# A routed layer whose next tokens are turned at the beginning of a slot instead of among its output products

## The chip, the cores and the metric

The kernel runs on one core of one Trainium2 chip. The metric is the device time of one execution in microseconds (us); the kernel before was run three times. Beside those runs one execution was taken by the hardware profiler; all rows below are from it, and their times count from the start of its span. Engines are called as in the profile: PE multiplies matrices, PEld loads its weights, DVE and ACT are the vector and the scalar engine, POOL is the general-purpose engine (here it mostly issues gathers and scatters), SP issues the other DMAs.

## What is computed

The reference chains three layers, all in float32. Only the third matters here, `x` being the 4608 tokens of 512 numbers that the second leaves:

```python
logits = x @ w_gate + modality_bias[modality_id]
e_idx = np.argmax(logits, axis=1)
...
for e in range(E):                       # E = 8 experts
    mask = e_idx == e
    ...
    h = np.maximum(x[mask] @ w1[e], 0.0) # 512 -> 1024
    out[mask] = gate_w[mask, None] * (h @ w2[e])   # 1024 -> 512
```

Before it stand a linear attention over 64 heads and a dense layer, `(h * cos(h)) @ w_out` with `h = x @ w_in`. Their code is the same in both kernels. A float32 product is made of three products of "high" and "low" parts: a tile is split by copying it to the type fp32r (the high part, ACT) and subtracting that from it (the low part, DVE).

## The kernel before

The dense layer runs over nine units of 512 tokens. For each unit the kernel also finds every token's expert, writes the token's number and its gate weight to a table in DRAM (`tab`, through `route2`, line 611: four indirect DMAs from POOL), and leaves the token's row in `x1d` in DRAM. In the table the tokens of one expert stand together.

The routed layer then works in slots, `body(i,w)` (line 770), each on 256 tokens of one expert. Slots 0 to 17 always run. After them come half slots of 128 tokens, `half(i)` (line 797), under branches on numbers that are known at run time (`small_slot`, `small_chain`, line 961 on); with this data the trace shows three, slots 18, 19 and 20, the last without any hooks.

What one full slot does:

- `prep` (line 760) has turned its tokens before it begins: eight 128x128 transposes on PE (tile `px`, line 767) put the gathered rows `xg` into two PSUM banks of the tag "nm" (`ms`, two banks that take turns), ACT copies each bank out as the high part `xT` (line 768), DVE subtracts for the low part (line 769).
- four steps of 24 products `mh` (line 782) of `w1` with `xT`; after each step ACT and DVE empty the bank into `hh` (line 784) and `hl` (line 785).
- eight steps of 6 products (two steps' worth of `hh`, `hl` with `w2` at a time, tile `po`, line 794). Each 128 tokens end with `finish` (line 834): ACT scales (`o`, line 836) and POOL scatters the rows to the output by an indirect DMA (line 837).

A half slot is 24 products `sh`, turns of its intermediate (`st`, emptied to `sg` by ACT and `sl` by DVE) and 24 products `sp`.

Two things happen ahead of time. The tokens of slot i+2 are fetched by `tokens(i+2)` in slot i: `gather` (line 755) loads a piece of the table from SP (`mrec`, line 757), and then issues two indirect DMAs from POOL (`xg`, line 759), one for 128 tokens. The weights of slot i+1 are loaded by `fetch` (line 724) and split by `split_steps` (line 735: `m`, ACT line 740, DVE line 741). The hooks of a slot say at which step these and `prep(i+1)` are called: `PLAN` (line 950) for the splits, the first step for `tokens(i+2)`, and `steps-3` for `prep(i+1)`. `steps` is 12 in a full slot and 8 in a half one.

The program text is not yet the order on an engine: the framework places each engine's instructions by its own planning, unless the code pins them (in half slots the products and the splits are pinned). An engine then runs its list in that order. Semaphores are counted by the framework; a buffer is taken again when its readers are done.

Of the kernel before, what the change touches and what calls it, by code (L numbers as in the profile page):

```python
# [28 lines left out]
def f32(ap):  # L29
    return ap.bitcast(F32)  # L30
# [315 lines left out]
def moes(tc, ctx, consts, S, ps, ident, att, end_att, xt, w_in, w_out, x1d, tab, wgt, w1, w2, out):  # L346
# [178 lines left out]
    def ms(name): return bank("nm",name)  # L525
# [42 lines left out]
    def rows(u,c):  # L568
        pr=ms(f"pr_{u}_{c}")
        for d in range(4):  # L570
            nc.tensor.transpose(pr[:,d*P:(d+1)*P],x1T[u,d][:,c*P:(c+1)*P],ident)
        t=xtile("row",f"row_{u}_{c}",F32)
        if c%2==0: nc.scalar.copy(t,pr)
        else: nc.vector.tensor_copy(t,pr)
        put(u,c,t)
# [35 lines left out]
    def route2(u):  # L611

        oh,ob,rec=ohs.pop(u)
        pk=ms(f"pk_{u}")
        for c in range(4):
            nc.tensor.matmul(pk[:,c*8:(c+1)*8],C["tri"],ob[:,c,:],start=True,stop=c==0)
            for c2 in range(c):
                nc.tensor.matmul(pk[:,c*8:(c+1)*8],C["one"],ob[:,c2,:],start=False,stop=c2==c-1)
        for c in range(4):
            nc.tensor.matmul(pk[:,32:40],C["one"],ob[:,c,:],start=c==0,stop=c==3)  # L620
        nr=C["pool"].tile([P,8],F32,tag="run",name=f"run_{u}",bufs=2)
        nc.vector.tensor_tensor(nr,pk[:,32:40],C["run"],ALU.add)
        r=small("r",u,[P,4,8])
        nc.vector.tensor_tensor(r,pk[:,0:32].rearrange("p (c e) -> p c e",e=8),C["run"].unsqueeze(1).to_broadcast([P,4,8]),ALU.add)
        C["run"]=nr
        nc.vector.tensor_tensor(r,r,oh,ALU.mult)
        ps=small("ps",u,[P,4]); nc.vector.tensor_reduce(ps,r,AX.X,ALU.add)
        pi=sb.tile([P,4],I32,tag="pi",name=f"pi_{u}",bufs=2); nc.vector.tensor_copy(pi,ps)
        for c in range(4):
            nc.gpsimd.indirect_dma_start(tab[:],IndirectOffsetOnAxis(ap=pi[:,c:c+1],axis=0),rec[:,c,:],None)  # L630
# [76 lines left out]
    def load_e(i):  # L707
        e_[i]=value(o["pe" if i<PRE else "e"][0:1,i:i+1],SP,NE-1,"an expert")
# [26 lines left out]
    def split_steps(i,which):  # L735

        for f in range(NF2):
            m=raw(i,which,f//2)
            h,l=W[i,which][f]; a=place(m)[:,(f%2)*512:(f%2+1)*512]
            keep(nc.scalar.copy(h,a))  # L740
            keep(nc.vector.tensor_tensor(l,a,f32(h),ALU.subtract))  # L741
            if f%2==1: fetch(m+(8 if i<=DEEP else 11))
            yield
    X={}
    R={}
    def alloc(i):
        X[i]=list(zip(*[pair("ke",f"xT_{i}_{g}",112) for g in range(2)]))
# [12 lines left out]
    def prep(i):  # L760

        h,l=X[i]; xg=xgs[i]
        for g in range(2):
            pt=ms(f"px_{i}_{g}")
            for d in range(2):
                for c in range(2):
                    nc.tensor.transpose(pt[:,d*T+c*P:d*T+(c+1)*P],xg[c][:,(2*g+d)*P:(2*g+d+1)*P],ident)
            nc.scalar.copy(h[g],pt)
            nc.vector.tensor_tensor(l[g],pt,f32(h[g]),ALU.subtract)
# [68 lines left out]
    def run(steps,hooks):  # L838

        n=0  # L840
        for _ in steps:
            for f in hooks.get(n,()): f()
            n+=1
        for f in hooks.get("end",()): f()


    LAG=3
# [1 line left out]
    def lg(d):  # L849
        def f(u): pend.append(logits(u,d))  # L850
        return f
# [59 lines left out]
    def tokens(i):  # L911
        if i<NS0+2: alloc_g(i)
        load_off(i); gather(i)
    def weights(m0,m1):
        for m in range(m0,m1): fetch(m)
    def hooks(i,steps):


        if i+1==NS1: return {}
        def ahead():  # L920
            if i+2<NS1: tokens(i+2)
        sp=[split_steps(i+1,w) for w in range(2)]
        def go(w):
            def f(): next(sp[w],None)
            return f
        h={n:[] for n in range(steps)}
        for n,(m0,m1) in enumerate(PLAN[steps]): h[n]+=[go(0)]*m0+[go(1)]*m1
        def start():
            if i<NS0: alloc(i+1)
            for j in (i+2,i+3):  # L930
                if j<NS1 and (i>1 or j<PRE): load_e(j)
        h[0].insert(0,start)
        if i==0: h[0].insert(0,lambda: (tokens(2),tokens(3)))
        elif i>1: h[0].insert(0,ahead)
        if i==DEEP:
            def more():
                for n in range(2): RAW.append(S("raw_k",f"raw_{8+n}",F32)[:,0:1024])
                RAW.append(spare[0][:,0:1024])
                weights(8*i+16,8*i+19)
            h[11].append(more)  # L940
        if i==0:
            for n,fs in {0:[lg(0)],1:[lg(1)],2:[lg(2)],3:[lg(3)],4:[pe,pe,pe,pe],6:[route1],7:[lambda u:rows(u,0)],8:[lambda u:rows(u,1)],
                         9:[lambda u:rows(u,2)],10:[lambda u:rows(u,3)]}.items():
                h[n]+=[(lambda f: lambda: f(u))(f) for f in fs]
        if i==1:
            h[1].append(lambda: route2(u))
            h[4].append(order)
        h[steps-3].append(lambda:prep(i+1))
        return h
    PLAN={12:((0,2),)*4+((2,0),)*4+((0,0),)*4,8:((0,2),(0,2),(2,0),(2,0),(2,0),(2,0),(0,2),(0,2))}  # L950
    for i in range(NS0):
        if i==NS0-1:
            loaded=[value(o["n"][0:1,j:j+1],mybir.ALL_ENGINES,NS1,"only compared with constants") for j in range(3+NSH)]
        run(body(i,i),hooks(i,12))
# [6 lines left out]
    def small_slot(i,last=False):  # L961
        pin.append(1); run(half(i),{} if last else hooks(i,8)); pin.pop()
# [11 lines left out]
    def slots(i):  # L974

        with tc.If(loaded[0]>i): run(body(i,i),hooks(i,12))
        with tc.If(loaded[2+i-NS0]>0): small_slot(i)
        if i+1<NS0+NSH: slots(i+1)
        else: small_slots(i+1)
# [93 lines left out]
```

## Time and profile before

| what | value |
|---|---|
| median of 3 runs | 1635.33 us (1635.13 to 1636.0) |
| the profiled execution's own time | 1632.78 us |
| its span, first to last instruction | 1630.7 us |
| PE busy | 1598.6 us, 98% of the span |
| DVE, ACT, POOL busy | 1147.1, 846.1, 408.5 us |
| first product `mh` of slot 0 | 1160.26 us |
| first product of half slot 18 | 1582.44 us |
| last product | 1624.74 us |

The profiled execution is 2.55 us shorter than the median and 2.08 us longer than its own span. A row of a timeline has the start, the length and the instruction; several alike in a row are merged, and in brackets stands how long the engine sat idle before and whose signal ended that. Lengths of merged products overlap a little, so the starts are the better measure.

### The profile page before, as it was taken

The numbers are of one execution on the slowest core, as the hardware profiler recorded it, in microseconds if no ns is written. First come the engines' busy times: TensorE is split into PE (matmuls) and PEld (weight loads), VectorE is DVE, ScalarE is ACT, GpSimd is POOL, SyncE is SP. The second block draws the span as 40 slices with busy tenths as digits, with TensorE's granted clock in tenths as the row PEclk, the third lists the DMA queues.
The fourth block names the chain that finished last, engine by engine and source line by source line (L and its number), as shares of the span: only waits on it lengthen the run. The fifth ranks groups of instructions, "written<-read, shape, count | busy, mean of one in ns | idle before, by whom it ended". The sixth has DMA issues, their size and how long they took to land.

```text
span 1630.7 us, 33696 instructions
## 1 busy us (share of the span) xinstructions
PE 1598.6 (98%) x13074; PEld 1370.5 (84%) x13076; DVE 1147.1 (70%) x2364; ACT 846.1 (52%) x1563; POOL 408.5 (25%) x336
## 2 busy tenths in 40 slices
PE   8999999989999999999999999999999999999997
PEld 6888888878788888888888888888899999999985
DVE  4888888889856758586777667674875656665645
ACT  4666676656533434343433434344765656565645
POOL 0000000022123334343344333343122112211212
PEclk9999999999999999999999999999999999999999
DMA  6644444423210101010100101004748667766656
GB/s 175 209 135 141 144 145 144 138 95 118 91 45 8 46 7 39 14 39 14 40 14 7 40 14 39 7 1 155 231 151 307 224 228 252 246 223 218 223 195 235
DMA packets 144831, 195.55 MB, mean 120 GB/s; under 512 B 64647, under 2 KB 89351, under 8 KB 144658
## 3 DMA queue, kind: packets, MB, share of 16 engines
q1 hardware_dynamic: 136866, 172.24, 33.4%
q0 software_dynamic: 7792, 21.02, 3.8%
q8 instruction: 107, 1.75, 0.5%
q14 instruction: 66, 0.54, 0.1%
HBM read 162.18 MB, written 31.82 MB: 119 GB/s over the span
## 4 chain that ended last, share of the span: by engine, by line
PE 72%; DVE 13%; ACT 6%; DMA 5%; issue 3%; POOL 0%; SPq 0%; DVEq 0%; POOLq 0%; ACTq 0%
PE ph L473 19%; PE acc L511 15%; PE mh L782 11%; PE po L794 10%; PE acc L516 4%; PE pj L136 4%; DMA out_dram<-o,mrec 3%; PE pn L210 2%; PE kv L174 2%; DVE x L463 2%; PE pt L121 1%; DVE t_k L142 1%; DVE m_k L141 1%; PE ptt L189 1%; DVE fr L488 1%
## 5 line engine op out<-in xcount | busy, mean ns | idle before, releaser
L473 PE MATMUL ph<-x,w 128*128 128x512 f32 x1728 | 422.6, 392 | 4.8 <-DVE x L463 3.7
L473 PEld LDWEIGHTS ph<-x,w 128*128 128x128 f32 x1728 | 322.3, 188 | 78.9 <-DVE x L463 6.4
L500 POOL TENSOR_TENSOR gl<-fr,gh 128x512 fp32r<-128x512 f32 x130 | 195.6, 1507 | 362.6 <-DVE gh L499 298.6
L741 DVE TENSOR_TENSOR m<-raw,m 128x512 fp32r<-128x512 f32 x320 | 207.9, 686 | 103.9 <-ACT m L740 102.9
L511 PE MATMUL acc<-w,gh 128*128 128x512 f32 x896 | 276.1, 389 | 0.0
L486 ACT ACTIVATE n<-ph 128x512 int32<-128x512 f32 x144 | 85.8, 596 | 258.2 <-PE ph L473 258.0
L740 ACT CAST m<-raw 128x512 fp32r<-128x512 f32 x320 | 187.7, 619 | 39.7 <-PE mh L782 32.5
L782 PEld LDWEIGHTS mh<-xT,m 128*128 128x128 f32 x1728 | 205.6, 189 | 2.5 <-DVE hl L785 1.0
L782 PE MATMUL mh<-xT,m 128*128 128x256 f32 x1728 | 206.6, 281 | 0.6 <-DVE hl L785 0.6
L511 PEld LDWEIGHTS acc<-w,gh 128*128 128x128 f32 x896 | 168.2, 188 | 35.1
L488 DVE SCALAR_TENSOR_TENSOR fr<-ph,n 128x512 f32<-128x512 f32 x144 | 99.1, 688 | 132.0 <-ACT n L486 118.7
L541 DVE SCALAR_TENSOR_TENSOR junk<-x1T,wg 128x512 f32<-128x512 f32 x224 | 179.8, 802 | 0.0
L794 PE MATMUL po<-m,hh 128*128 128x512 f32 x576 | 179.6, 393 | 0.0
L490 ACT ACTIVATE fr<-fr 128x512 f32<-128x512 f32 x144 | 91.1, 633 | 160.6 <-DVE fr L488 159.9
L511 PE MATMUL acc<-w,gl 128*128 128x512 f32 x448 | 174.4, 389 | 0.0
L493 DVE SCALAR_TENSOR_TENSOR fr<-fr,ph 128x512 f32<-128x512 f32 x144 | 98.6, 685 | 69.9 <-ACT fr L491 69.9
L794 PEld LDWEIGHTS po<-m,hh 128*128 128x128 f32 x576 | 105.2, 188 | 19.6
L794 PE MATMUL po<-m,hl 128*128 128x512 f32 x288 | 112.4, 390 | 0.0
L837 POOL DMA_INDIRECT out_dram<-o,mrec x39 | 43.1, 1105 | 274.2 <-ACT o L836 259.3
L511 PEld LDWEIGHTS acc<-w,gl 128*128 128x128 f32 x448 | 84.1, 188 | 17.5
L491 ACT ACTIVATE fr<-fr 128x512 f32<-128x512 f32 x144 | 90.9, 632 | 4.0
L141 DVE TENSOR_REDUCE m_q<-pj 128x4 f32<-128x512 f32 (+1 forms) x80 | 50.9, 637 | 58.5 <-PE pj L136 58.5
(215 smaller groups left out, 2385.4 us busy)
## 6 DMA issues: line engine op xcount, KB each, us to landing
raw<-in_moe_w_dram SPq DMA_DIRECT2D x170, 512.0 KB, 5.8
xt<-xo SPq DMA_DIRECT2D x16, 576.0 KB, 3.9
xr<-xt SPq DMA_DIRECT2D x36, 256.0 KB, 3.1
raw_k<-in_k_dram SPq DMA_DIRECT2D x32, 256.0 KB, 2.9
raw_q<-in_q_dram SPq DMA_DIRECT2D x32, 256.0 KB, 3.7
v<-in_v_dram SPq DMA_DIRECT2D x64, 128.0 KB, 3.1
st<-in_moe_w_in_dram SPq DMA_DIRECT2D x16, 512.0 KB, 4.4
st<-in_moe_w_out_dram SPq DMA_DIRECT2D x16, 512.0 KB, 3.8
```

Source lines behind the costliest of these rows:

```text
L473: nc.tensor.matmul(ph,A[:,ws],xhl[u,d][k],start=n[0]==0,stop=n[0]==11); n[0]+=1
L488: nc.vector.scalar_tensor_tensor(g,ph,INV2PI,n,op0=ALU.mult,op1=ALU.subtract)
L490: nc.scalar.activation(g,g,AF.Sin,scale=math.pi)
L491: nc.scalar.activation(g,g,AF.Square)
L493: nc.vector.scalar_tensor_tensor(g,g,-0.5,ph,op0=ALU.add,op1=ALU.mult)
L500: nc.gpsimd.tensor_tensor(gl,g,f32(gh),ALU.subtract)
L511: nc.tensor.matmul(accs[u][c],A[:,ws],B,start=(f==0 and k==0),stop=(f==NF-1 and k==2))
L541: return lambda: tc.keep_in_program_order(nc.vector.scalar_tensor_tensor(junk,x1T[u,c],1.0,wg[e],op0=ALU.mult,op1=ALU.mult,accum_out=lgs[u ...
L740: keep(nc.scalar.copy(h,a))
L741: keep(nc.vector.tensor_tensor(l,a,f32(h),ALU.subtract))
L782: nc.tensor.matmul(ph[:,f2*T:(f2+1)*T],A[:,ws],B[d//2][:,xs],start=n==0,stop=n==11); n+=1
L794: nc.tensor.matmul(po[c],A[:,ws],B,start=(f==0 and j==0),stop=(f==NF2-1 and j==2))
```

## The change

`prep(i+1)` is no longer called at step `steps-3`. It is called once, before the slot's first product is issued, together with the allocation of its tiles and the register loads of the expert numbers, by a new hook "begin". Full and half slots are both changed. The unused hook "end" goes.

```diff
@@ def run(steps,hooks):
         n=0
+        for f in hooks.get("begin",()): f()
         for _ in steps:
             for f in hooks.get(n,()): f()
             n+=1
-        for f in hooks.get("end",()): f()
@@ def hooks(i,steps):
         def start():
             if i<NS0: alloc(i+1)
             for j in (i+2,i+3):
                 if j<NS1 and (i>1 or j<PRE): load_e(j)
-        h[0].insert(0,start)
+            prep(i+1)
+        h["begin"]=[start]
...
-        h[steps-3].append(lambda:prep(i+1))
         return h
```

What this does on PE at the border of half slots 18 and 19, from the middle of slot 18's output products (`sp`) to the first products of slot 19 (`sh`). `px_0`, `px_1` are the turns of the next slot's tokens, `xg_0`, `xg_1` the two gathered tiles; the wait DMASW is for an indirect DMA. Before:

```order
L767 MATMUL px_0_17882<-ident,xg_0_17551 128x128 [waits DMASW3_49,PE_49]
L767 MATMUL px_0_17882<-ident,xg_1_17552 128x128 [waits DMASW4_49]
...
L800 MATMUL sp_17834<-m_4_12845,sl_1_17852 128x512 [waits DVE_49]
...
L767 MATMUL px_1_17889<-ident,xg_0_17551 128x128 [waits PE_49]
...
L800 MATMUL sp_17834<-m_7_12848,sl_1_17852 128x512
L966 COMPARE_AND_BRANCH
L800 MATMUL sh_0_17918<-m_0_12833,xT_0_17768 128x512 [waits Activation_49]
L800 MATMUL sh_0_17918<-m_0_12833,xT_0_17768 128x512 [waits DVE_49]
```

and with the change:

```order
L800 MATMUL sp_17848<-m_4_12845,sl_1_17866 128x512 [waits DVE_49]
...
L800 MATMUL sp_17848<-m_7_12848,sl_1_17866 128x512
L966 COMPARE_AND_BRANCH
L767 MATMUL px_0_17924<-ident,xg_0_17284 128x128 [waits DMASW0_49,PE_49]
L767 MATMUL px_0_17924<-ident,xg_1_17285 128x128 [waits DMASW1_49]
...
L767 MATMUL px_1_17931<-ident,xg_0_17284 128x128 [waits PE_49]
...
L800 MATMUL sh_0_17938<-m_0_12833,xT_0_17768 128x512 x3
```

The turns in the first list are of slot 19's tokens; those of the second, behind the branch, are of slot 20's, which slot 18 gathers. They now stand in front of all of slot 19's products, and the two waits for the gathers with them.

On POOL the order changes at one place, in slot 2: `o_0` and `o_1` are rows of slot 1 on their way out, `xg_0`, `xg_1` the tokens of slot 4 (their turns stand in slot 3). Before:

```order
L837 DMA out_dram<-o_0_13716,mrec_12580 4608x512 [waits DMASW6_49,DMASW1_49,Activation_49]
L759 DMA xg_0_13799<-x1d,mrec_13798 128x512 [waits DMAHW5_49,DMAHW3_49,DMAHW6_49,DMAHW2_49,DMAHW7_49,DMASW7_49,PE_49]
L759 DMA xg_1_13800<-x1d,mrec_13798 128x512 [waits PE_49]
L837 DMA out_dram<-o_1_13764,mrec_12580 4608x512 [waits DMASW6_49,Activation_49]
L837 DMA out_dram<-o_0_13963,mrec_13138 4608x512 [waits DMASW1_49,Activation_49]
```

and with the change:

```order
L837 DMA out_dram<-o_0_13730,mrec_12580 4608x512 [waits DMASW6_49,DMASW1_49,Activation_49]
L759 DMA xg_0_13821<-x1d,mrec_13820 128x512 [waits DMAHW5_49,DMAHW3_49,DMAHW6_49,DMAHW2_49,DMAHW7_49,DMASW7_49,PE_49]
L837 DMA out_dram<-o_1_13764,mrec_12580 4608x512 [waits DMASW6_49,Activation_49]
L759 DMA xg_1_13822<-x1d,mrec_13820 128x512 [waits PE_49]
L837 DMA out_dram<-o_0_13977,mrec_13160 4608x512 [waits DMASW0_49,Activation_49]
```

The second gather and the scatter have changed places. In all later slots POOL's order is the same in both kernels, the gathers of half slot 18 included. On ACT and DVE the two copies and the two subtractions of `xT` move with the turns, to just before the slot's first `hh` (or `sr`, the first result in a half slot).

## Rows read from the trace of the kernel before

**Rows 1.** The page, part 1: busy time, share of the span, instructions.

```profile
PE 1598.6 (98%) x13074; PEld 1370.5 (84%) x13076; DVE 1147.1 (70%) x2364; ACT 846.1 (52%) x1563; POOL 408.5 (25%) x336
```

**Rows 2.** Busy time by stretch: length, PE, PEld, DVE, ACT, POOL; granted clock, DMA share, GB/s.

```profile
1160.26:1189.03 28.77, 28.37 (x185) 23.91 (x184) 24.54 (x49) 21.95 (x41) 5.96 (x5) 1.00 0.82 285
...
1559.36:1582.44 23.08, 23.08 (x153) 21.15 (x152) 10.48 (x17) 9.62 (x18) 4.69 (x4) 1.00 0.60 201
1582.44:1595.81 13.37, 13.28 (x65) 10.52 (x64) 7.94 (x13) 10.06 (x20) 3.24 (x3) 1.00 0.45 149
1595.81:1612.97 17.16, 13.69 (x65) 10.29 (x64) 14.86 (x26) 14.67 (x29) 6.63 (x4) 1.00 0.95 318
```

**Rows 3.** PE's timeline, the turns in slot 2 and the border to slot 3.

```profile
1231.85 1.04 PE L767 MATMUL px<-ident,xg 128*128 128x128 f32 x8
1232.64 0.71 PE L794 MATMUL po<-m,hh 128*128 128x512 f32 x2
...
1235.46 0.75 PE L782 MATMUL mh<-xT,m 128*128 128x256 f32 x5
```

**Rows 4.** POOL's timeline, slot 19's tokens gathered at the end of slot 16.

```profile
1559.08 1.47 POOL L759 DMA_INDIRECT xg<-x1d,mrec  x1 [3.89 <-PE po L794]
```

**Rows 5.** All instructions on the tile xg: time from issue to landing.

```profile
DMA to landing us min/median/max: 3.4/6.2/8.4
```

**Rows 6.** POOL's timeline, slots 1 and 2: table written, slot 4's tokens gathered.

```profile
1197.92 1.23 POOL L630 DMA_INDIRECT tab<-rec,pi  x1 [6.71 <-DVE srt L670]
...
1226.86 0.99 POOL L759 DMA_INDIRECT xg<-x1d,mrec  x1 [5.20 <-DMA mrec<-tab]
1228.15 0.97 POOL L759 DMA_INDIRECT xg<-x1d,mrec  x1 [0.30 <-issue]
1229.42 1.03 POOL L837 DMA_INDIRECT out_dram<-o,mrec  x1 [0.30 <-issue]
```

**Rows 7.** DMA issues of 1228.1 to 1229.15 us: KB each and us to landing.

```profile
xg<-x1d,mrec POOLq DMA_INDIRECT x1, 7.3
```

**Rows 8.** POOL's timeline, half slot 18: slot 20's tokens gathered.

```profile
1588.48 0.99 POOL L759 DMA_INDIRECT xg<-x1d,mrec  x1 [3.85 <-DVE m L741]
1593.07 1.27 POOL L759 DMA_INDIRECT xg<-x1d,mrec  x1 [3.60 <-DMA out_dram<-o,mrec]
```

**Rows 9.** DMA issues of 1593 to 1594.1 us.

```profile
xg<-x1d,mrec POOLq DMA_INDIRECT x1, 7.9
```

**Rows 10.** PE's timeline, half slots 18 and 19 and the start of 20.

```profile
1592.42 0.60 PE L767 MATMUL px<-ident,xg 128*128 128x128 f32 x4
1592.94 0.50 PE L800 MATMUL sp<-m,sl 128*128 128x512 f32 x1
...
1595.81 0.39 PE L800 MATMUL sh<-m,xT 128*128 128x512 f32 x1
1597.16 1.19 PE L800 MATMUL sh<-m,xT 128*128 128x512 f32 x4 [0.96 <-DVE xT L769]
...
1612.97 0.47 PE L800 MATMUL sh<-m,xT 128*128 128x512 f32 x1 [2.41 <-ACT m L740]
```

**Rows 11.** Line 966, the branches behind half slots: PE's sequencer, ns min/median/max.

```profile
L966 PEldq COMPARE_BRANCH  x3: 65/3467/5201, 1593.0 to 1622.4; - x3
```

**Rows 12.** PE's timeline, the program's start and its last product.

```profile
12.64 1.23 PE L136 MATMUL pj<-w,qT 64*128 64x128 f32 x8 [1.10 <-DVE t_k L142]
...
15.91 1.06 PE L121 MATMUL pt<-ident,raw_k 128*128 128x128 f32 x4
...
17.65 0.66 PE L189 MATMUL ptt<-ident,t_q 128*128 128x128 f32 x4
...
1624.74 0.39 PE L800 MATMUL sp<-m,sl 128*128 128x512 f32 x1
```

**Rows 13.** Busy time by stretch, columns as in rows 2, behind the last product.

```profile
1628.50:1630.70 2.20, 0.00 (x0) 0.00 (x0) 0.00 (x0) 0.00 (x0) 0.00 (x0) 0.50 0.00 0
```

**Rows 14.** DVE's timeline at the beginning of slot 0.

```profile
1159.63 1.28 DVE L769 TENSOR_TENSOR xT<-px,xT 128x512 fp32r<-128x512 f32 x2
```

## The prediction, made before the changed kernel was run

> **What bounds the kernel now.** I read the page's busy times first, then busy time by stretch, one for each slot at the end of the routed layer, then PE's own timeline across the borders of slots, and last POOL's timeline with the times from issue to landing, because the step that moves is the one step on PE that reads gathered tokens.
>
> PE is busy for 98% of the span [rows 1], and a full slot is the plainest case: slot 17 lasts 23.08 us, of which PE is busy 23.08 [rows 2]. In the same stretch DVE and ACT work 10.48 and 9.62 us. So in full slots nothing that these two do can make the time shorter; only PE work that goes away, or a wait that comes, can change it. PE's idle time in the routed layer lies at its two ends. Slot 0 has 28.37 us of PE in 28.77. Half slot 19 has 13.69 in 17.16 [rows 2]: 0.96 us at its first products, put down to the low part of `xT` on DVE, and 2.41 us before slot 20 [rows 10], put down to a copy on ACT; but the branch in front of slot 20 is the longest of three on PE's sequencer, 5201 ns [rows 11], and I take that for the cause.
>
> **The change part by part.**
>
> *The turns themselves.* Eight transposes a slot, with their four evacuations, are neither added nor removed. In slot 2 they take from 1231.85 to 1232.64, that is 0.79 us of PE [rows 3]. They go from the output products to the front of the same slot, so over a full slot PE does the same work: 0 for 17 of the 18 slots apart from what follows. Unknown is the edge to other neighbours (products of 256 columns behind them and not of 512); I bound it by 0.1 us a slot either way, an eighth of the turns' own time, 1.7 us in all, and take 0. The copies and subtractions of `xT` leave the second half of the slot and come before `hh`, with half of DVE and ACT idle: 0.
>
> *Slot 0.* Its banks for the turns of slot 1 are still being emptied from slot 0's own turns: DVE's two subtractions run from 1159.63 for 1.28 us, to 1160.91 [rows 14], while PE reaches the slot at 1160.26 [rows 2]. That is a new wait of at most 0.65 us. Against it stand the 0.40 us that PE idles in this slot now [rows 2], part of which is for work of DVE that gets further ahead. I take 0, with 0.7 either way.
>
> *The gathers, which the turns wait for.* Before, the turns of slot i+1 stood some 18 us into slot i. Now PE stops at the front of slot i until they have landed, and everything of the slot is queued behind. In an ordinary slot that is covered: the tokens of slot 19 are issued from 1559.08 [rows 4], they land 3.4 to 8.4 us later [rows 5], and would be wanted at 1582.44 [rows 2], some 14 us after. Two places have no such cover.
>
> *Slot 3 wants slot 4's tokens.* Their two gathers are issued at 1226.86 and 1228.15 [rows 6], late because the piece of the table is read only after the table's last writes, a chain that starts at 1197.92 [rows 6]. The second takes 7.3 us [rows 7] and so lands at 1235.45; slot 3 begins at 1235.46 [rows 3]. Nothing is left over, and the change takes more. On POOL the second gather now stands behind a scatter and takes its place, 1229.42 [rows 6], 1.27 later. And the table's writes follow products of slot 1 that now stand behind 0.79 us of turns. So landing comes at 1229.42 + 0.79 + 7.3 = 1237.5, against 1235.46: a wait of **2.0 us**. Low end 0 (the fastest landing, 3.4 [rows 5], in place of 7.3). High end about 5: landing 8.4 instead of 7.3, and 2 us for the chain of table writes, whose four steps I saw once.
>
> *Half slots 18 and 19.* In slot 18 the first half of the turns now fills a hole: it starts at 1592.42, while the next product waits for DVE's `sl` until 1592.94 [rows 10]. Moved, the first half costs its full time at the front, and the hole stays. The second half, 0.4 us, goes from behind that wait. So the wait for `sl` ends 0.79 later, at 1593.73, and what remains to the slot's end is 1595.81 - 1592.94 - 0.4 = 2.47 us: slot 18 ends at 1596.2, 0.4 later than now. Slot 19 then wants slot 20's tokens, which slot 18 fetches. Their second gather is issued at 1593.07 [rows 8] and takes 7.9 us [rows 9]: 1600.97. PE waits 4.8 us, and then turns for 0.79, so its first product runs at 1601.76 and the second some 0.2 later, at 1602.0. Now it is 1597.16 [rows 10]. The wait of 0.96 us for `xT` is gone within that: the difference is **4.8 us**. Behind that point both chains are alike up to the branch, and what the second half of the turns covered of it (0.4 us) is given back by their absence. Low end: landing 3.4 instead of 7.9, that is +0.3. High end: landing 8.4 and an issue 1.5 later, +6.8.
>
> *The clock.* A wait of 4.8 us is longer than any that PE has in the routed layer now. The idle 2.41 us in slot 19 left the granted clock at 1.00 [rows 2, 10]. Behind the last product, which ends at 1625.13 [rows 12], it is 0.50 by 1628.50 [rows 13], that is 1.2 instead of 2.4 GHz. The 4.8 us lie beyond that, so I expect slot 19 to begin at the lower level. What it takes to get back I read from the program's start: four transposes take 1.06 us at 15.91 and 0.66 at 17.65, and PE has worked nearly without a stop since 12.64 [rows 12]. 5.0 us at half speed lose **2.5 us**. Low end 0, high end 5 (slot 3 as well).
>
> The Trainium skill, "TensorE: Matmul & The Clock Gate", section "Why this matters for your kernels", warns of idle gaps of PE between bursts of matmuls, since they put the clock back to its half; the clock in the rows falls behind the last product, which agrees, and no row here shows a PE pause of 4.8 us inside the program. By that rule the sum is as below; without a fall it would be 1642.1.
>
> **Sum.** 2.0 + 4.8 + 2.5 = 9.3 us. The profiled execution, 1632.78 (a span of 1630.7 and 2.08 around it), would become 1642.1. It stands 2.55 below the median of the runs, 1635.33, which becomes **1644.6**, 0.57% more.
>
> **The rivals.**
>
> *The gathers are in time* (no change to speak of). The 3.60 us before the second gather of slot 18 have no cause that I can name: the row blames a scatter, while in slot 2 the second follows after 1.29 [rows 6, 8]. Issued 1.29 after the first, at 1589.77, it would land by 1597.7 and PE would wait 1.5 instead of 4.8, without a fall of the clock: 1.5 + 2.0 from slot 3, 1638.8; with slot 3 in time too, 1636.8. Against it: POOL's order in slot 18 is the same as before and what releases it is not moved. I give 1636.8, since these are mostly within 0.2%.
>
> *Faster.* This is what is bought if the gathers cost nothing: the wait for `xT`, 0.96 us, and, if the row is right that ACT and not the branch ends the 2.41 us before slot 20 [rows 10], those too, because two copies less then stand in front of the splits. 3.4 us together: 1632.0. It decides if slot 20's tokens land before 1596.2, 4.8 us earlier than in the trace. That they take 7.9 of at most 8.4 us speaks for some room, but 3.4 at best [rows 5] brings it no lower than 1596.5.
>
> *Worse.* The waits grow on each other: the table's chain in slot 1 slips, slot 3 waits 5 us, and the clock falls there as well. 5 + 2.5 + 6.8 + 2.5, less nothing: 16.8, that is 1652.1. For it speaks that every landing here shares the queues with weight loads.
>
> That the turns do not move is excluded by the order on PE.
>
> **Chances.** Forecast (both waits or slot 19's alone, with or without the clock, +3.3 to +14): 0.69. In time: 0.15. Faster: 0.04. Worse: 0.12. The range that leaves out a fifth runs from 1637.5 (one short wait) to 1651.0 (the forecast's terms near their high ends). A measurement of this kernel can tell about 0.2%, 3.3 us, from no change. Faster by more than that 0.03; within it 0.15, the rival in time with half of the faster one lying inside; slower 0.82.
>
> **What would show it.** PE's timeline has `px` first in each slot. Right: an idle stretch of 4 to 5 us before `px` at the front of slot 19, ended by the DMA on `xg`, with a granted clock below 1 in the stretch behind it; another of 1 to 3 us at the front of slot 3; slots 4 to 17 at 23.1 us; no wait for `xT` in slot 19, and still one of over 2 us before slot 20. Wrong: if slot 20's second gather is issued well before 1593 or lands within 4 us; if the 2.41 us before slot 20 shrink together with ACT's load; or if full slots change by more than 0.1 us each.

## The result and the profile after

The changed kernel takes 1644.66 us (median of 7 runs, 1638.74 to 1646.86), the kernel before 1635.33 in the same comparison (7 runs, 1632.97 to 1636.3). The ratio is 1.0054, with a 95% interval of 1.0039 to 1.0068: between 6.4 and 11.1 us slower, about 8.8. The forecast was 1644.6. It hit the median more closely than its terms deserve, as the sum below shows.

The profiled execution of the changed kernel also takes 1644.66 us, with a span of 1642.6. That is 11.9 more than the span before, and more than the runs show, since the profiled execution before stood 2.55 below its median and this one stands on it.

PE does the same 13074 instructions, and is busy for 3.0 us longer than before [rows 1]. Part 1 of the page after:

```profile
PE 1601.6 (98%) x13074; PEld 1372.6 (84%) x13076; DVE 1150.3 (70%) x2364; ACT 846.4 (52%) x1563; POOL 404.8 (25%) x336
```

Busy time by stretch, columns as in [rows 2], of slots 0, 3, 17, 18 and 19. Each now begins with its turns:

```profile
1161.07:1190.26 29.19, 28.34 (x185) 24.03 (x185) 24.66 (x48) 21.69 (x41) 5.77 (x5) 1.00 0.82 271
...
1236.50:1264.13 27.63, 24.50 (x154) 22.30 (x153) 14.24 (x23) 14.16 (x25) 6.10 (x6) 0.94 0.77 284
...
1565.21:1588.31 23.10, 23.10 (x154) 21.16 (x153) 10.32 (x17) 9.52 (x18) 3.98 (x4) 1.00 0.63 214
1588.31:1602.10 13.79, 13.36 (x65) 10.47 (x64) 8.85 (x15) 10.68 (x21) 3.04 (x3) 1.00 0.45 139
1602.10:1624.74 22.64, 15.08 (x66) 11.46 (x64) 15.51 (x26) 14.50 (x28) 6.46 (x4) 0.92 0.79 265
```

The first number is a slot's length, the second PE's busy time in it. Slot 17 is as long as before. Slot 3 and slot 19 stand out, and in both the granted clock is below 1. Set against the rows before, the 11.9 us lie here:

| stretch | before | after | difference |
|---|---|---|---|
| start of the span to slot 0 | 1160.26 | 1161.07 | +0.81 |
| slots 0 to 2 | 75.20 | 75.43 | +0.23 |
| slots 3 to 17 | 346.98 | 351.81 | +4.83 |
| slot 18 | 13.37 | 13.79 | +0.42 |
| slot 19 | 17.16 | 22.64 | +5.48 |
| slot 20 to the end of the span | 17.73 | 17.86 | +0.13 |

Of the 4.83 in the third line slot 3 alone has 27.63 - 23.08 = 4.55; the 14 slots behind it share 0.28, that is 0.02 each.

PE's timeline of the changed kernel at the front of slots 3, 19 and 20, and in slot 18:

```profile
1236.50 0.27 PE L767 MATMUL px<-ident,xg 128*128 128x128 f32 x1
1239.90 0.98 PE L767 MATMUL px<-ident,xg 128*128 128x128 f32 x7 [3.13 <-DMA xg<-x1d,mrec]
...
1589.10 4.38 PE L800 MATMUL sh<-m,xT 128*128 128x512 f32 x18
...
1599.68 0.50 PE L800 MATMUL sp<-m,sl 128*128 128x512 f32 x1 [0.35 <-DVE sl L816]
...
1602.10 0.27 PE L767 MATMUL px<-ident,xg 128*128 128x128 f32 x1
1606.62 1.75 PE L767 MATMUL px<-ident,xg 128*128 128x128 f32 x7 [4.24 <-DMA xg<-x1d,mrec]
1608.02 5.06 PE L800 MATMUL sh<-m,xT 128*128 128x512 f32 x18
...
1624.74 4.41 PE L800 MATMUL sh<-m,xT 128*128 128x512 f32 x18 [2.87 <-issue]
```

At both places the first turn, which reads the first gathered tile, goes through; the second turn reads the other tile and waits, 3.13 us at slot 3 and 4.24 at slot 19, and the releaser is the gather's landing. Behind the second wait 18 products take 5.06 us, and 4.38 in slot 18. Busy time by stretch behind the two waits shows why, in the column before the last two:

```profile
1240.90:1244.20 3.30, 3.30 (x17) 3.30 (x17) 1.89 (x3) 1.17 (x3) 0.34 (x1) 0.50 1.04 377
1244.30:1248.00 3.70, 3.70 (x34) 3.70 (x34) 1.19 (x2) 1.75 (x4) 2.53 (x3) 1.00 1.05 392
1606.10:1609.40 3.30, 2.79 (x10) 2.54 (x11) 1.07 (x2) 1.17 (x2) 0.43 (x1) 0.50 1.06 412
```

Behind each wait the clock is granted at half, 1.2 GHz, for some 3.4 us: 17 products in 3.3 us, against 34 in the 3.7 us that follow.

The split between waiting and clock can now be read from busy and idle time. In slot 3 PE is busy for 24.50 us against 23.08 in a plain slot (+1.42, the clock) and idle for 3.13. In slot 19 it is busy for 15.08 against 13.69 before (+1.39, the clock) and idle for 7.56 against 3.47 (+4.09). The idle part is made of the new wait, +4.24; the wait for `xT`, 0.96, which is gone; 0.35 for `sl`, as in slot 18's row, which the turns used to fill; and 0.46 more before slot 20.

Last the two second gathers. POOL's timeline in slots 1 and 2, and in slot 18:

```profile
1199.88 1.24 POOL L630 DMA_INDIRECT tab<-rec,pi  x1 [7.43 <-DVE srt L670]
...
1228.83 1.00 POOL L759 DMA_INDIRECT xg<-x1d,mrec  x1 [6.38 <-DMA mrec<-tab]
1230.13 1.01 POOL L837 DMA_INDIRECT out_dram<-o,mrec  x1 [0.30 <-issue]
1231.44 0.99 POOL L759 DMA_INDIRECT xg<-x1d,mrec  x1 [0.30 <-PE po L794]
...
1594.35 1.09 POOL L759 DMA_INDIRECT xg<-x1d,mrec  x1 [3.85 <-DVE m L741]
1598.93 0.97 POOL L759 DMA_INDIRECT xg<-x1d,mrec  x1 [3.50 <-DMA out_dram<-o,mrec]
```

and the issues of 1231.44 and of 1598.93 with their time to landing:

```profile
xg<-x1d,mrec POOLq DMA_INDIRECT x1, 8.4
...
xg<-x1d,mrec POOLq DMA_INDIRECT x1, 7.6
```

1231.44 + 8.4 and 1598.93 + 7.6 are 1239.84 and 1606.53, within 0.1 us of the restart of PE at 1239.90 and 1606.62.

### The profile page after: what moved, and what is told of

The parts are those of the page before. It is cut to its first block, busy times and chain, and to the rows that moved or that the text cites. A ratio compares the mean times of both kernels' runs of the same rounds, so it can differ in the third digit from the quotient of the medians.

```text
span 1642.6 us, 33682 instructions
## 1 busy us (share of the span) xinstructions
PE 1601.6 (98%) x13074; PEld 1372.6 (84%) x13076; DVE 1150.3 (70%) x2364; ACT 846.4 (52%) x1563; POOL 404.8 (25%) x336
## 4 chain that ended last, share of the span: by engine, by line
PE 70%; DVE 12%; ACT 7%; DMA 6%; issue 3%; SPq 2%; POOL 0%; DVEq 0%; POOLq 0%; ACTq 0%
PE ph L473 19%; PE acc L511 14%; PE mh L782 11%; PE po L794 10%; PE acc L516 4%; PE pj L136 3%; DMA out_dram<-o,mrec 3%; PE pn L210 3%; PE kv L174 2%; DVE x L463 2%; DVE t_k L142 1%; PE pt L121 1%; DVE m_k L141 1%; DVE fr L488 1%; ACT qx L195 1%
```

## The experiments

The theory was that the two waits, with the fall of the clock behind each, are the whole cost, and that moving the turns costs nothing where the tokens have landed. Its rivals: the half slots alone cost (A); every full slot pays for turns at its front (B); the lower clock costs nothing (C); what precedes slot 20 is ACT's work, so that a gain is hidden there (D). Each difference below is of medians, against runs of the kernel before on the same chip. [rows 2] and the profile after are what the traces are held against.

**Full slots only, half slots only, full slots without slot 3.** The three kernels call `prep(i+1)` at the beginning where the condition holds, and at `steps-3` elsewhere:

```diff
+            if steps==12: prep(i+1)            # full slots only
+            if steps==8: prep(i+1)             # half slots only
+            if steps==12 and i!=3: prep(i+1)   # full slots without slot 3
```

> Turns at the beginning in full slots only; half slots as before. Theory (the two waits for gathered tokens, at the front of slot 3 and of half slot 19, with a fall of the clock behind each, are the whole cost): only slot 3's part is left, a pause of about 3 us before px and some 1.4 us of lower clock, so +4 us against the kernel before (3 to 5.5); slots 4 to 17 at 23.1 us, slot 19's front as before. Rival A (the half slots alone cost, and slot 3's pause is made up later): 0, within 1 us. Rival B (each full slot pays for turns at its front): the loss is spread over the slots, +0.2 us or more in each of slots 4 to 17, +6 or more in all.

Measured: 1638.85 against 1634.74, +4.1 us, ratio 1.0020 (1.0007 to 1.0033). PE's timeline at its slot 3:

```profile
1237.04 0.33 PE L767 MATMUL px<-ident,xg 128*128 128x128 f32 x1 [0.46 <-DMA xg<-x1d,mrec]
1239.86 1.75 PE L767 MATMUL px<-ident,xg 128*128 128x128 f32 x7 [2.49 <-DMA xg<-x1d,mrec]
```

> Turns at the beginning in half slots only; full slots as before. Theory (two waits for gathered tokens): slot 19's part alone, 4.2 us of waiting, some 1.4 of lower clock and 0.4 in slot 18, less nothing: +5.9 us against the kernel before (5 to 7); no pause at slot 3. Rival A (the half slots alone cost): the whole of the change, +9. Rival B (each full slot pays): +3 or less.

Measured: 1642.21 against 1634.74, +7.5 us, ratio 1.0042 (1.0029 to 1.0055, that is 4.7 to 9.0 us). That is more than the 5 to 7 that were expected, though the interval reaches down to there. PE's timeline at its slot 19, and two stretches behind it:

```profile
1602.27 1.76 PE L767 MATMUL px<-ident,xg 128*128 128x128 f32 x7 [3.89 <-DMA xg<-x1d,mrec]
1603.67 6.22 PE L800 MATMUL sh<-m,xT 128*128 128x512 f32 x18
```

```profile
1600.80:1607.60 6.80, 5.33 (x16) 4.53 (x17) 2.21 (x4) 1.17 (x2) 1.73 (x1) 0.50 0.98 374
...
1621.30:1624.60 3.30, 3.09 (x7) 2.48 (x8) 0.77 (x2) 0.00 (x0) 1.67 (x1) 0.50 0.98 358
```

The wait itself is shorter than in the change, 3.89 us. But here the clock stayed at half twice as long, for 6.8 us, so the 18 products take 6.22 and not 5.06 us, and it fell once more at slot 20. The place of the loss was right, the price of the clock was not.

> Turns at the beginning in all full slots but slot 3; slot 3 and the half slots as before. Theory (two waits): neither place is touched, so the time of the kernel before, 0 within 1 us, with 17 slots' turns moved. Rival B (each full slot pays for turns at its front): +3 or more, spread over slots 4 to 17. A gain of over 1 us would mean that the move itself is good for something in full slots that the trace does not show.

Measured: 1634.6 against 1634.74, ratio 0.9998 (0.9989 to 1.0008). Slots 5 to 16 as one stretch, of this kernel and then of the kernel before:

```profile
1282.47:1560.39 277.92, 277.47 (x1825) 253.78 (x1824) 170.22 (x265) 163.97 (x289) 50.32 (x47) 1.00 0.69 233
```

```profile
1281.63:1559.36 277.73, 277.13 (x1826) 253.66 (x1824) 167.96 (x265) 163.86 (x289) 50.29 (x48) 1.00 0.70 234
```

Twelve slots with moved turns are longer by 0.19 us in all. Rival B falls: turns at the front of a full slot are free where their tokens have landed. Rival A falls by the first kernel: 4.1 us without a half slot changed. The two parts, 0.0020 and 0.0042, make 0.0062 together, and the whole change is 0.0054, within the intervals.

**PE kept busy during the waits.**

```diff
+            fill={3:12,19:18}.get(i,0)
+            if fill:
+                pw=ms(f"fill_{i}"); xw=X[i][0][0]
+                for j in range(fill): tc.keep_in_program_order(nc.tensor.matmul(pw,xw[:,0:P],xw,start=j==0,stop=j==fill-1))
+            prep(i+1)
```

> The change, and beside it products whose results nothing uses, right ahead of the turns at the front of slot 3 (12 of 128x512, about 2.6 us) and of slot 19 (18, about 3.9 us), so that PE works while it would wait. Theory (waits and, behind each, a clock at half for 3.4 us): the waits stay in length, nearly filled, and the granted clock stays at 1.00 behind both; the two losses of about 1.4 us go, so 2.8 us less than the change, about +6 us against the kernel before (5 to 7.5). Rival C (the lower clock in the records costs nothing, since what follows waits for something else): no less than the change, +9.

Measured: 1640.08 against 1634.74, +5.3 us, ratio 1.0040 (1.0027 to 1.0054). PE's timeline at slots 3 and 19:

```profile
1235.24 2.90 PE L935 MATMUL fill<-xT 128*128 128x512 f32 x12
1237.98 1.03 PE L767 MATMUL px<-ident,xg 128*128 128x128 f32 x8
...
1593.74 4.26 PE L935 MATMUL fill<-xT 128*128 128x512 f32 x18
1597.84 1.07 PE L767 MATMUL px<-ident,xg 128*128 128x128 f32 x8
1598.66 4.37 PE L800 MATMUL sh<-m,xT 128*128 128x512 f32 x18
...
1615.48 6.94 PE L800 MATMUL sh<-m,xT 128*128 128x512 f32 x18 [3.63 <-issue]
```

and busy time by stretch over the fillers, the turns and what follows:

```profile
1234.80:1244.80 10.00, 10.00 (x74) 9.39 (x73) 4.88 (x9) 4.75 (x10) 2.48 (x3) 1.00 1.04 401
1593.70:1607.00 13.30, 13.30 (x68) 11.00 (x68) 7.81 (x14) 7.64 (x16) 3.89 (x2) 1.00 0.79 271
```

PE begins the turns almost as late as the second turn of the change (2.74 and 4.10 us into the slot, behind the fillers, and not 3.40 and 4.52), but the clock stays at 1.00, the eight turns take 0.8 us and the 18 products 4.37 again. From the turns to the end of slot 19's last product it now takes 14.0 us, and 15.2 behind the wait in the change. So rival C falls in the trace: the lower clock costs, and nothing later in the slot makes it up. The medians don't show it by themselves: those of the change and of this kernel, from two comparisons, lie 4.6 us apart, the ratios 2.3, and the intervals of the ratios overlap. In this execution the clock fell at another place instead, behind the pause of 3.63 us before slot 20, where 18 products take 6.94 us.

**Slot 20's tokens one slot earlier.** The turns are at the beginning everywhere but in slot 3; `tokens(20)` is called in slot 17 and not in slot 18.

```diff
-            if i+2<NS1: tokens(i+2)
+            if i+2<NS1 and i!=NS0: tokens(i+2)
+            if i==NS0-1:
+                xgs[NS0+2]=xgs[NS0]
+                R[NS0+2]=sb.tile([P,2,2],I32,tag="mrec",name=f"mrec_{NS0+2}",bufs=4)
+                tokens(NS0+2)
...
+            if i!=3: prep(i+1)
```

> Turns at the beginning of every slot but slot 3, half slots too, and slot 20's tokens gathered one slot earlier, in slot 17, so that they lie there long before slot 19 begins. Theory (the two waits for gathered tokens are the whole cost): both are gone and no fall of the clock; slot 19's old wait of 0.96 us for xT is gone too, against 0.4 more in slot 18: 0 against the kernel before, within 1.2 us either way, no pause before px anywhere over 0.6 us, and still over 2 us before slot 20 by the branch. Rival A (the half slots cost for another reason, such as the turns standing ahead of the products): +4 or more, with slot 19's gather long landed. Rival D (the time before slot 20 is ACT's work, not the branch, and shrinks once the copies of xT are out of the way): -2 or less.

Measured: 1634.39 against 1634.96, ratio 0.9999 (0.9989 to 1.0008). POOL's timeline in slot 17, PE's at slots 19 and 20, and the stretches of slots 19 and 18:

```profile
1566.84 0.97 POOL L759 DMA_INDIRECT xg<-x1d,mrec  x1 [5.34 <-PE mh L782]
1568.12 0.96 POOL L759 DMA_INDIRECT xg<-x1d,mrec  x1 [0.30 <-PE mh L782]
```

```profile
1593.65 1.03 PE L767 MATMUL px<-ident,xg 128*128 128x128 f32 x8
...
1610.32 4.40 PE L800 MATMUL sh<-m,xT 128*128 128x512 f32 x18 [2.75 <-issue]
```

```profile
1593.65:1610.32 16.67, 13.48 (x65) 10.33 (x63) 15.17 (x26) 14.34 (x28) 7.08 (x4) 1.00 0.91 305
1579.87:1593.65 13.78, 13.33 (x66) 10.48 (x65) 8.84 (x15) 10.68 (x21) 1.17 (x1) 1.00 0.42 137
```

With the tokens landed the turns of slot 19 run in one piece, without a wait, and the two half slots last 13.78 + 16.67 = 30.45 us, against 30.53 before [rows 2]. So in half slots too it is the landing that costs and not the place. Rival D falls: the copies of `xT` are away from the splits, and PE still idles 2.75 us before slot 20. ACT's timeline has its last two copies of the splits there:

```profile
1608.53 1.13 ACT L740 CAST m<-raw 128x512 fp32r<-128x512 f32 x2
```

They end at 1609.66, and PE starts 0.66 us later, at 1610.32.

**Turns one step later.** `h[1].append(lambda:prep(i+1))` in place of the call at the beginning, in every slot.

> Turns one step later than in the change, behind the first products of each slot (24 in a full slot, some 18 in a half one), everything else as in the change. Theory (waits for landings): the first products cover 5.5 us at slot 3 and 4 us at slot 19, so the pause at slot 3 (3.1) goes and that at slot 19 shrinks to 0.5 us or less, with no fall of the clock: +0.5 us against the kernel before (-0.7 to 1.5). Rival A or B (the place of the turns costs by itself, by half slots or by all slots): +4 or more. Rival D (before slot 20 ACT decides): -2 or less.

Measured: 1634.45 against 1634.96, ratio 0.9995 (0.9986 to 1.0004). PE's timeline in slots 3 and 19:

```profile
1235.33 5.82 PE L782 MATMUL mh<-xT,m 128*128 128x256 f32 x48
1240.99 1.03 PE L767 MATMUL px<-ident,xg 128*128 128x128 f32 x8
...
1602.38 1.03 PE L767 MATMUL px<-ident,xg 128*128 128x128 f32 x8
1605.73 0.66 PE L813 MATMUL st<-ident,sr 128*128 128x128 f32 x4 [0.92 <-DVE xT L769]
```

On PE the turns end up behind 48 products in slot 3, which is two of its steps and not one, and behind all 24 products `sh` in slot 19. These cover both landings; slot 3 lasts 23.09 us. The second gathers are issued about as late as in the change, 5.64 us ahead of slot 3 (5.06 there) and 3.36 ahead of slot 19 (3.17 there), and cost nothing. In half slots a new small wait of 0.92 comes. Neither this kernel nor the previous one, with slot 20's tokens a slot earlier, can be told from the kernel before by its time.

**The scatter between slot 4's gathers.** The change, with slot 1's two scatters held back to step 2 of slot 2:

```diff
+        if i==1: held.append(scatter)
+        else: scatter()
...
+        if i==2: h[2].append(lambda: [f() for f in held])
```

On POOL this moves only the second one, behind both gathers.

> The change, with one thing else: on POOL, slot 1's second scatter is held back until both gathers of slot 4's tokens are issued in slot 2, so these follow each other as in the kernel before. Theory (slot 3's pause is made of the scatter between the gathers, 1.3 us, of a first gather that is issued later than before, and of the landing): the second gather follows the first by 1.29 us and not 2.61, and the pause before px at the front of slot 3 shrinks from 3.13 to about 1.8 us (0.5 to 3, as landings spread), with or without a fall of the clock behind it; slot 19's pause stays at about 4.2. Against the kernel before +7 us (5 to 9). Rival E (the scatter is not in the way; the first gather or the table sets the landing): the pause stays at 3 us or more, +9. Rival F (the scatter is all of it): no pause at slot 3, +5.9.

Measured: 1641.69 against 1634.49, +7.2 us, ratio 1.0043 (1.0029 to 1.0057). POOL's timeline in slot 2 and PE's at slot 3:

```profile
1226.85 0.99 POOL L759 DMA_INDIRECT xg<-x1d,mrec  x1 [6.82 <-DMA mrec<-tab]
1228.14 0.97 POOL L759 DMA_INDIRECT xg<-x1d,mrec  x1 [0.30 <-issue]
```

```profile
1235.59 0.98 PE L767 MATMUL px<-ident,xg 128*128 128x128 f32 x7 [1.15 <-DMA xg<-x1d,mrec]
```

The gathers follow each other by 1.29 us and the pause shrinks from 3.13 to 1.15; slot 3 lasts 24.52 us and not 27.63, with the clock at 1.00 throughout. Only about half of that is the scatter's: the second gather is issued 5.97 us ahead of slot 3 and not 5.06, and it lands after 7.4 us and not 8.4, which can be chance. The scatter was in the way, and it was not all of it: by the trace rivals E and F both fall. The times don't separate them, as the interval, 4.7 to 9.3 us, holds the 9 of E and the 5.9 of F.

## Why the prediction was right

*Full slots, 0 forecast.* Right: 0.02 us a slot in the change, 0.19 in twelve slots in the kernel that moves only them. One reading beside it was off: slot 2 begins at 1212.37 in the profile before, so its turns [rows 3] stood 19.5 us into it and not some 18. No term of the sum uses that.

*Slot 0, 0 forecast.* Slot 0 is 0.42 us longer, and slots 0 to 2 together 0.23, within the 0.7 given.

*Slot 3, 2.0 forecast.* The mechanism was right, the term mis-sized: 3.13 us. The shift of the table's writes was 0.79 in the forecast; the first write is issued 1.96 later than before [rows 6], and slot 1 begins 1.23 later, which leaves 0.73. At the first gather, 1.97 later than before with slot 3 beginning 1.04 later, it is 0.93. The scatter was 1.27 and is 1.31. The landing was taken at 7.3, as before [rows 7], and took 8.4: that is most of the missing 1.1 us. It was in the range, as the slowest landing of [rows 5]. That this landing spreads fits the 12 runs of the kernel with full slots alone, which lie between 1632.48 and 1641.81.

*Half slots, 4.8 forecast.* Slot 18 is 0.42 longer (forecast 0.4). The second gather is issued 10.62 us after the slot's beginning, before 10.63, and lands after 7.6 us instead of 7.9. With what was gained and lost inside slot 19, +4.09 and +0.42 make 4.5.

*The clock, 2.5 forecast.* The size was nearly right, the shape wrong. I expected one fall, of 5.0 us, in slot 19. There were two, of some 3.4 us, one at each wait; they cost 1.42 and 1.39, that is 2.8. "Slot 3 as well" stood in the forecast only as the high end. The step that failed there is the argument from length, that what lies beyond 2.41 us falls and what is shorter doesn't; see the last section.

*The sum.* 9.3 forecast, 3.13 + 4.5 + 2.8 = 10.4 in the profile. The 1.1 of the landing is the difference. The medians lie 9.3 apart and the ratio says 8.8, so the hit to a tenth of a microsecond is luck: the runs of the change spread over 8 us. The remaining 1.5 us of the 11.9 are mostly the 0.81 ahead of slot 0. There the clock was at half for a while at the first products of the dense layer, whose code is the same. The changed kernel starts these at 355.52, 0.83 us earlier than before (356.35), and is 0.81 later at slot 0:

```profile
352.00:362.00 10.00, 7.34 (x39) 5.45 (x38) 6.51 (x15) 3.91 (x6) 2.84 (x3) 0.83 0.55 195
```

In the profile before the clock is 1.00 in that stretch. It fell there in four of the nine profiles and not in the other five, among them the kernel with fillers and the one with the late scatter, which move the same turns.

*The rivals.* "In time" and "faster" fell by the two waits; "faster" also by its price, as PE still stood for 2.87 us before slot 20 while ACT's copies of `xT` had gone. The longest branch on PE's sequencer is as long as before [rows 11]. Its row in the change (ns, first and last start):

```profile
L966 PEldq COMPARE_BRANCH  x1: 5328/5328/5328, 1619.4 to 1619.4; - x1
```

It ends at 1624.7, where slot 20's first product starts (1624.74). That fits the forecast's choice of the branch as the cause; why the branch takes so long no run here shows.

"Worse" foresaw the second fall of the clock, but not the sizes.

## What to carry to other kernels

Before a step is moved ahead, ask when what it reads has landed in the slots that differ from the rest: the first ones behind a late table, and the last ones, which are shorter. The ordinary slots, with some 14 us to spare, tell nothing about the two that have none. And where a short wait in front of an engine that is otherwise full can't be avoided, put some of its own work ahead of the waiting step: 48 products in slot 3 and 24 in slot 19 removed the whole cost here, without an earlier gather.

## What the runs showed of the hardware that was not expected

*The length of a pause between 2 and 3 us does not tell whether PE's clock falls.* The pause before slot 20 was 2.08 us in the kernel with the turns one step later, and the clock was at half behind it; it was 2.87 in the change, and the clock stayed. Busy time by stretch, of the first and then of the change:

```profile
1614.10:1617.40 3.30, 3.30 (x9) 2.61 (x8) 0.00 (x0) 0.07 (x1) 0.00 (x0) 0.50 0.98 354
```

```profile
1624.80:1628.10 3.30, 3.30 (x15) 2.70 (x16) 0.46 (x1) 0.24 (x1) 1.36 (x1) 1.00 0.95 320
```

Nine products against fifteen in 3.3 us. The same holds for one pause and the same code: the 2.65 us ahead of the dense layer's first products stand in all nine profiles, within 0.02, and the clock fell behind them in four. Behind the pause before slot 20 it fell in five of the nine, so part of a difference between two single executions can be that fall and not the kernel. The Trainium skill, "TensorE: Matmul & The Clock Gate", section "Why this matters for your kernels", warns of long idle gaps between bursts of matmuls; the pauses of 3.13, 3.89 and 4.24 us agree, and that of 2.08 us shows that a shorter one can be followed by a fall as well. So the price of a wait of 2 to 4 us was the wait and beside it nothing, 1.4 or 2.5 us (the busy time added in slot 19 of the change, and of the kernel with half slots only, where 16.22 stands against 13.69):

```profile
1598.10:1621.51 23.41, 16.22 (x65) 12.29 (x64) 15.45 (x26) 14.50 (x28) 6.59 (x4) 0.85 0.76 258
```

*In slot 18, the first slot behind a branch, POOL's two gathers come slowly.* The second gather is issued 4.6 us after the first in every profile where it stands there (1598.93 - 1594.35 in the change); the same two gathers in slot 17, ahead of the branch, are 1.28 apart. A branch ahead of them is not enough to explain it, since the two gathers of slot 19, behind the next branch, are 1.28 apart in the change (1614.68 and 1615.96). Nor is it plainly a wait for the first gather's data: these land 4.6 us after their issue, at 1598.95, while POOL's sequencer goes on with a register move at 1598.7. But the two times lie close together. Instructions that arrive late would be another cause; no run here separates the causes, and it stays open. What is shown is the price of gathering there: a slot earlier the tokens are in time, and the whole loss of the half slots is gone. That the slow second gather alone makes this loss is not shown. Without the 3.3 us that it stands too far behind, the wait of 4.24 us would be about 0.9, an estimate from these times if the landing stays the same.
